# Splitting the last w2 rows of a one-token gated mix thirteen and five instead of eight and ten

## The chip, the cores and the metric

The kernel runs on one NeuronCore of one Trainium2 chip. The metric is device time in microseconds of one execution. Before the change the median of three runs is 131.49 us (131.48 to 131.57). Engines are named as in the profile: PE is TensorE, PEld its weight loads, DVE VectorE, ACT ScalarE, POOL GpSimd, SP SyncE, which here issues the large loads.

## The reference

One token `x` of 576 numbers goes through two branches, and a gate mixes them:

```python
g = sigmoid((x * gate_w).sum(-1, keepdims=True))
a = attention(x)                       # 32 heads over 16 kv heads, last 4096 keys of the cache
b = gelu(x @ w1 + b1) @ w2 + b2        # 576 -> 4608 -> 576
return g * a + (1 - g) * b
```

Inside `a`, the query is `x @ wq` (576 by 4096), the keys and values are the last 4096 positions of a cache, and the heads' outputs go through `wo` (4096 by 576). All inputs are bf16. With one token there is almost no reuse: each weight and each cache entry is read once, some 53.6 MB in all, and multiplied by a vector.

## The kernel before, in words

Everything is loaded through SP's queue in one fixed order: `w1`, `wq`, four K blocks and four V blocks of 4 MB, `wo`, then `w2`. The stages follow the loads: the first MLP layer, the query, scores and softmax per group of four kv heads, the value products, then the output projection.

The output projection is what the change touches. A "row" is a tile of 128 input features by 576 outputs; the vector that multiplies it is one column of 128 numbers (`ov` for `wo`, `gt` for `w2`, where the gate `1 - g` is already multiplied in). `wo` has 31 rows plus a four-row remainder. `w2` has `NF = 36` rows: the first half, 18 rows, comes in one load (L776), the second half in four loads (L778): rows 0 to 9, rows 10 to 14, rows 15 and 16, and row 17, counted within the second half. Row numbers below are these, 0 to 17.

A row can be added in two ways:

- `y_add` (the matmul is L389) multiplies a one-column weight by 288 outputs, twice, once per half of the 576 outputs. The two halves stand in partition 0 and partition 32 of one PSUM tile, `y_ps`. That is two weight loads and two matmuls a row.
- `y_end` (L852) writes into two other banks, `end_a` (152 columns, partitions 0 and 1) and `end_b` (136 columns, partitions 32 and 33). There the two output halves stand in two neighbouring partitions. Its weights are two columns of `g_late`, in which the column of `gt` alternates with a zero column, so that each matmul fills one partition and adds zeros to the other. A row takes four weight loads and four matmuls.

The last `LATE` rows of `w2` go through `y_end`, the others through `y_add`. When the last `y_add` is done, DVE copies `y_ps` to SBUF (`y_kept`, L845), and `y_carry` (L864) adds that copy to `end_a` and `end_b` with one f32 matmul each, which the program executes as two passes of a weight load and a matmul. At the end ACT casts `end_a` (L880), DVE casts `end_b` (L881) into `out_rows`, and SP stores the 576 numbers (L882).

The order on PE is written out by hand: `queue("pe", ...)` puts every step behind the one before. Three dummy f32 products into a spare bank (L832) stand between the stages of the projection; the last, with 256 columns, stands ahead of the second half of `w2`. SP's loads have no order against PE but through semaphores: the first matmul of each load's rows waits for that load.

The lines that set the order of the last rows:

```python
late += [(gt, f, w2_t[:, f, :]) for f in range(NJ, NF - LATE)]    # y_add
...
for j in range(LATE):
    if j == 5:
        queue("pe", y_carry)
    queue("pe", lambda: y_end(j))                                 # row NF - LATE + j
```

`g_late` has `2 * LATE + 2` columns; POOL clears it and copies the last `LATE` columns of `gt` into every second one (L480, L481).

Of the kernel before, what the change touches and what calls it, by code (L numbers as in the profile page):

```python
# [18 lines left out]
def kernel(  # L19
# [31 lines left out]
    QH = Hq * Dh // 2  # L51
    DH = D // 2
    DA = 152
    LATE = 8
    SCALE = 1.0 / (Dh**0.5)

    def first_load_ahead(nc):
# [420 lines left out]
    )  # L478
    g_late = const.tile([P, 2 * LATE + 2], BF16, name="g_late")
    nc.gpsimd.memset(g_late[:].bitcast(FP32), 0.0)  # L480
    nc.gpsimd.tensor_copy(out=g_late[:, 1 : 2 * LATE : 2], in_=gt[:, NF - LATE : NF])  # L481
    pick = const.tile([33, 2], FP32, name="pick")
# [343 lines left out]
    late += [256]  # L826
    late += [(gt, f, w2_t[:, f, :]) for f in range(NJ, NF - LATE)]
    for n, item in enumerate(late):
# [20 lines left out]
    def y_end(j):  # L849
        for s in range(2):  # L850
            for c0, c1, to in ends:
                last = nc.tensor.matmul(  # L852
                    to,
                    lhsT=g_late[:, 2 * j + 1 - s : 2 * j + 3 - s],
                    rhs=w2_t[:, NF - LATE + j, DH * s + c0 : DH * s + c1],
                    start=(j == 0 and s == 0),
                    stop=(j == LATE - 1 and s == 1),
                    skip_group_check=True,
# [14 lines left out]

    for j in range(LATE):
        if j == 5:
# [37 lines left out]
```

## Time and profile before

| | |
|---|---|
| median of 3 runs | 131.49 us |
| the profiled execution | 131.65 us |
| its span, first to last instruction | 130.4 us |
| DMA packets, bytes, mean rate | 2506, 53.69 MB, 412 GB/s |
| PE busy | 82.2 us (63%) |
| PEld busy | 26.1 us (20%) |
| DVE busy | 61.3 us (47%) |
| ACT busy, POOL busy | 11.4 us (9%), 10.5 us (8%) |
| mean granted TensorE clock | 0.869 |
| granted clock from 120 us to the end | 1.00 |

Times in the profile are counted from the span's start. Busy shares are means over stages with different limits. For the last five microseconds the table says nothing; there the timeline and the chain of waits must be read. "Landing" of a load is the moment when its semaphore has its full value, that is when the last of the 16 DMA engines has reported.

### The profile page before, as it was taken

How to read it: one execution, taken by the hardware profiler on the slowest of the kernel's cores; microseconds unless marked ns; L12 is line 12 of the kernel's file. 1: busy time of each engine (PE TensorE's matmuls, PEld its weight loads, DVE VectorE, ACT ScalarE, POOL GpSimd, SP SyncE). 2: the span in 40 equal slices, each digit the busy share in tenths (PEclk: the TensorE clock that was granted, in tenths of full speed). 3: DMA queues.
4: the chain of work that ended last, by engine and by line, in shares of the span. 5: the costliest groups of instructions: out<-in, count | busy, mean ns of one | idle time of the engine just before them, and what ended most of it. 6: DMA issues, size and time to landing. Idle time of an engine off the chain costs nothing.

```text
span 130.4 us, 1195 instructions
## 1 busy us (share of the span) xinstructions
PE 82.2 (63%) x562; PEld 26.1 (20%) x436; DVE 61.3 (47%) x51; ACT 11.4 (9%) x27; POOL 10.5 (8%) x36
## 2 busy tenths in 40 slices
PE   0003999497106998679739958951085074789995
PEld 0003111310100221211201202321032021325543
DVE  0030003416199689999999994559005005100001
ACT  3032100210300000030020003030000000000000
POOL 7019800020000000000000000000100000000000
PEclk9999999999755699999995999999658757756999
DMA  7999999899899989989989999999999989999970
GB/s 249 409 438 431 468 441 464 372 452 462 382 442 472 437 372 472 442 382 472 442 372 472 452 392 442 452 397 432 455 405 432 484 373 482 399 407 404 408 294 12
DMA packets 2506, 53.69 MB, mean 412 GB/s; under 512 B 287, under 2 KB 420, under 8 KB 710
## 3 DMA queue, kind: packets, MB, share of 16 engines
q1 hardware_dynamic: 2492, 53.61, 96.2%
q8 instruction: 4, 0.07, 0.2%
q10 hardware_dynamic: 10, 0.01, 0.0%
HBM read 53.62 MB, written 0.00 MB: 411 GB/s over the span
## 4 chain that ended last, share of the span: by engine, by line
DMA 78%; DVE 11%; PE 7%; SPq 2%; issue 0%
DMA w_t<-in_B_w_dram 29%; DMA k_t<-in_A_k_cache_dram 26%; DMA v_t<-in_A_v_cache_dram 22%; DVE kt L567 10%; PE s_ps L589 4%; PE s_ps L682 1%; DVE m L605 1%; PE end_a L852 1%; SPq L776 0%; SPq L772 0%; PE end_b L852 0%; SPq L239 0%; SPq L778 0%; SPq L235 0%; DVE out_rows L881 0%
## 5 line engine op out<-in xcount | busy, mean ns | idle before, releaser
L589 PE MATMUL s_ps<-kt,qz_flat 128*128 128x512 bf16 x128 | 32.6, 412 | 12.6 <-DVE kt L567 7.6
L567 DVE STREAM_TRANSPOSE kt<-k_t 128x4096 f32<-128x4096 f32 x8 | 35.3, 4427 | 4.3 <-DMA k_t<-in_A_k_cache_dram 2.8
L682 PE MATMUL s_ps<-v_t,pt 128*32 128x512 bf16 x96 | 9.1, 547 | 10.0 <-DMA v_t<-in_A_v_cache_dram 10.0
L589 PEld LDWEIGHTS <-qz_flat 128*128 128x128 bf16 x64 | 6.8, 107 | 35.7 <-issue 35.4
L696 DVE TENSOR_TENSOR own<-s_ps,is 128x512 f32<-128x512 f32 x3 | 2.1, 687 | 16.0 <-PE s_ps L682 16.0
L626 ACT ACTIVATE p_t<-s_ps,negm 128x1024 bf16<-128x1024 f32 x4 | 4.5, 1113 | 46.9 <-DVE negm L622 46.9
L410 PE MATMUL s_ps<-w_t,x 128*32 128x512 bf16 x36 | 6.5, 623 | 1.6 <-DVE x L352 1.6
L845 DVE COPY y_kept<-y_ps 33x288 f32<-33x288 f32 x1 | 0.5, 450 | 14.8 <-PE y_ps L389 14.8
L344 PE MATMUL xs_ps<-ident,rows 1*128 1x1 bf16 x9 | 0.6, 189 | 10.7 <-POOL ident masks.py:199 10.7
L682 PEld LDWEIGHTS <-pt 128*32 128x32 bf16 x128 | 3.7, 118 | 15.5 <-DMA v_t<-in_A_v_cache_dram 10.3
L435 DVE STREAM_TRANSPOSE turned<-s_ps 128x1024 f32<-128x1024 f32 x2 | 2.5, 1250 | 8.3 <-PE s_ps L410 8.3
L389 PE MATMUL y_ps<-wo_t,ov 128*1 128x288 bf16 x62 | 5.8, 366 | 0.6 <-DMA wo_t<-in_A_wo_dram 0.6
L638 DVE STREAM_TRANSPOSE pt<-p_t 128x1024 bf16<-128x1024 bf16 x4 | 4.9, 1224 | 2.7 <-ACT p_t L626 2.7
L410 PE MATMUL s_ps<-wq_t,x 128*32 128x512 bf16 x36 | 5.1, 624 | 0.9 <-DMA wq_t<-in_A_wq_dram 0.9
L605 DVE TENSOR_REDUCE m<-s_ps 128x1 f32<-128x1024 f32 x4 | 4.8, 1194 | 0.7 <-PE s_ps L589 0.7
L717 PE MATMUL mt_ps<-is,summed 128*128 128x8 f32 x8 | 1.8, 293 | 5.2 <-DVE summed L706 5.2
L733 POOL TENSOR_TENSOR ls<-is,sums 128x32 f32<-128x32 f32 x1 | 0.2, 243 | 58.0 <-ACT p_t L626 58.0
L358 DVE CUSTOM_DVE_ANT_0 rows<-rows 1x576 bf16<-1x576 bf16 x1 | 0.7, 745 | 8.2 <-DMA rows<-in_gate_w_dram 8.2
L389 PEld LDWEIGHTS <-ov 128*1 128x1 bf16 x62 | 3.4, 105 | 4.3 <-issue 2.1
L706 DVE TENSOR_REDUCE summed<-own 128x128 f32<-128x512 f32 x4 | 4.1, 1018 | 0.1
L832 PE MATMUL s_ps<-p_t,ones 128*128 128x512 f32 (+1 forms) x6 | 3.9, 738 | 0.0
L389 PE MATMUL y_ps<-w_t,gt 128*1 128x288 bf16 x56 | 3.8, 286 | 0.0
(95 smaller groups left out, 58.8 us busy)
## 6 DMA issues: line engine op xcount, KB each, us to landing
k_t<-in_A_k_cache_dram SPq DMA_DIRECT2D x4, 4096.0 KB, 33.0
v_t<-in_A_v_cache_dram SPq DMA_DIRECT2D x4, 4096.0 KB, 17.7
wq_t<-in_A_wq_dram SPq DMA_DIRECT2D x1, 4608.0 KB
wo_t<-in_A_wo_dram SPq DMA_DIRECT2D x1, 4464.0 KB, 28.5
w_t<-in_B_w_dram SPq DMA_DIRECT2D x1, 2880.0 KB, 14.3
w_t<-in_B_w_dram SPq DMA_DIRECT2D x1, 2592.0 KB
w_t<-in_B_w_dram SPq DMA_DIRECT2D x1, 2304.0 KB, 8.2
w_t<-in_B_w_dram SPq DMA_DIRECT2D x1, 1440.0 KB
```

Source lines behind the costliest of these rows:

```text
L389: last = nc.tensor.matmul(y_ps[32 * s : 32 * s + wide, :], lhsT=vec, rhs=row[:, DH * s : DH * s + DH], start=start, stop=stop, skip_group_ ...
L410: nc.tensor.matmul(last[n][32 * g : 32 * g + 32], lhsT=vec, rhs=part(n), start=start and g0 == 0, stop=g0 + 4 + g >= len(pieces), skip_gro ...
L435: nc.vector.transpose(out=turned[:, c0 : c0 + n], in_=src[:].rearrange("p (q l j) -> p q j l", q=q, l=32),)
L567: lambda: nc.vector.transpose(out=kt[g, f][:].bitcast(FP32), in_=keys.rearrange("p c d -> p (c d)").bitcast(FP32),),
L589: last = nc.tensor.matmul(s_ps[g][:, u * 512 : (u + 1) * 512].rearrange("p (c k) -> p c k", k=32), lhsT=qz(g, j, 2 * f + half), rhs=kv[:, ...
L605: queue("dve", lambda: nc.vector.reduce_max(out=m1[:], in_=s_ps[g][:], axis=AX.X))
L626: nc.scalar.activation(out=p_t[:].rearrange("p c k -> p (c k)"), in_=s_ps[g][:], func=ACT.Exp, bias=negm[:, 0:1], scale=SCALE, accum_out=s ...
L638: lambda: nc.vector.transpose(out=pt[:, g, :, :].rearrange("p c q -> p (c q)"), in_=p_t[:].rearrange("p c k -> p (c k)"),),
L682: last = nc.tensor.matmul(acc[g][32 * (c % 4) : 32 * (c % 4) + 32, :], lhsT=pt[:, g, c, :], rhs=v_t[g][:, c:NCK:32, :], start=(c < 4), sto ...
L696: lambda: nc.vector.tensor_tensor(out=own[:], in0=acc[g].rearrange("p (c d) -> p c d", c=4), in1=same_c.rearrange("p (c o) -> p c o", o=1) ...
L706: lambda: nc.vector.tensor_reduce(out=summed[g][:], in_=own[:].rearrange("p c d -> p d c"), axis=AX.X, op=ALU.add,),
L832: lambda: nc.tensor.matmul(spare[:, 0:item], lhsT=ones[:], rhs=p_t[:].rearrange("p c k -> p (c k)").bitcast(FP32)[:, 0:item], start=True, ...
```

## The change

Thirteen instead of eight of the last `w2` rows go to `end_a` and `end_b`.

```diff
-    LATE = 8
+    LATE = 13
```

With that, rows 0 to 4 go through `y_add` and rows 5 to 17 through `y_end`. The copy of `y_ps` stands behind row 4 and not row 9. The carry stays behind the first five `y_end` rows, which are now rows 5 to 9 and were rows 10 to 14; so it stands ahead of row 10 and not ahead of row 15. `g_late` has 28 columns and not 18, and POOL copies 13 columns into it and not 8. The loads, their sizes and their order stay as they are.

## The prediction

> **What bounds the kernel now.** I read the page's table of engines and slices first, then the chain of waits to its end, then the timeline of the last five microseconds, then stretches of it. The page:
>
> ```profile
> span 130.4 us, 1195 instructions
> PE 82.2 (63%) x562; PEld 26.1 (20%) x436; DVE 61.3 (47%) x51; ACT 11.4 (9%) x27; POOL 10.5 (8%) x36
> DMA  7999999899899989989989999999999989999970
> DMA 78%; DVE 11%; PE 7%; SPq 2%; issue 0%
> ```
>
> The loads run nearly without a pause until the last slice but one, and the chain that ended last is 78% loads. The change touches no load, so all that it can move is what stands behind the last loads. The chain's end, in order of time (start, length, what):
>
> ```profile
> 88.97 38.14 DMA w_t<-in_B_w_dram
> 127.10 0.04 issue
> 127.15 0.22 PE end_a L852
> ...
> 127.97 0.21 PE end_a L864
> 128.18 0.12 PE end_b L864
> 128.29 0.02 PE end_a L864
> 128.31 0.15 PE end_a L852
> ...
> 128.87 0.29 DVE out_rows L881
> ```
>
> The load of rows 10 to 14 lands at 127.10, PE starts on it at 127.15, and from there to the end nothing but PE, the cast and the store is on the chain: no load is waited for again. The carry (L864) is on it. The timeline of these instructions (start, length, engine, line, what, count, idle before it):
>
> ```profile
> 125.46 1.39 PE L389 MATMUL y_ps<-w_t,gt 128*1 128x288 bf16 x20
> 126.89 0.45 DVE L845 COPY y_kept<-y_ps 33x288 f32<-33x288 f32 x1 [14.78 <-PE y_ps L389]
> 127.14 0.61 PEld L852 LDWEIGHTS <-g_late 128*2 128x2 bf16 x20 [0.62 <-DMA w_t<-in_B_w_dram]
> 127.74 0.23 PE L852 MATMUL end_a<-w_t,g_late 128*2 128x152 bf16 x1
> 127.89 0.08 PEld L864 LDWEIGHTS end_a<-y_kept,pick 33*2 33x2 f32 x2
> 128.24 0.35 PEld L852 LDWEIGHTS <-g_late 128*2 128x2 bf16 x12 [0.26 <-issue]
> 128.50 0.23 PE L852 MATMUL end_a<-w_t,g_late 128*2 128x152 bf16 x1
> ```
>
> PE is out of work before 127.15, waiting for rows 10 to 14. The last of their matmuls starts at 127.74; without the carry the next row would start at about 127.80, but row 15 starts at 128.24 and row 17 at 128.50. The copy had ended at 127.34, so the carry at 127.89 waited for nothing but its turn. Were the later rows there already? The load of rows 15 and 16 is issued at 94.98 and the list of loads gives 32.8 us to landing, 127.79. For row 17 no view prints a landing, since nobody waited for it; the trace's record of that load's semaphore has its sixteenth rise at 128.13. The stretches agree (length, busy times, granted clock, DMA share, GB/s):
>
> ```profile
> 127.40:127.60 0.20, 0.20 (x13) 0.20 (x9) 0.00 (x0) 0.00 (x0) 0.00 (x0) 1.00 0.06 23
> 127.60:127.70 0.10, 0.10 (x11) 0.10 (x5) 0.00 (x0) 0.00 (x0) 0.00 (x0) 1.00 0.04 12
> 127.70:128.20 0.50, 0.50 (x13) 0.15 (x6) 0.00 (x0) 0.00 (x0) 0.00 (x0) 1.00 0.00 0
> 128.20:129.10 0.90, 0.60 (x14) 0.35 (x12) 0.23 (x1) 0.27 (x1) 0.00 (x0) 1.00 0.06 18
> ```
>
> The last weight bytes move before 127.70, at a share of 0.04 to 0.06, which is one engine of sixteen (1/16 is 0.0625). So from 127.79 the bound is PE, 0.3 to 0.4 us behind the loads, with the carry in its way.
>
> **The change part by part.** All times are those of the profiled execution (131.65 us; span 130.4). The median shown is 0.16 below it; I take the difference in time over to the median.
>
> *Steps on PE.* A `y_add` row steps on by 0.122 (ten rows: the first pair starts at 125.46, the last at 126.56, nine steps). A `y_end` row steps on by 0.13 (rows 10 to 14 start from 127.15 to 127.67, four steps; 128.24 to 128.50 for two rows). From a first `y_end` to the carry behind five rows it is 0.75 (127.15 to 127.90), 0.65 of it rows and 0.10 the change over to f32 weights. The carry holds PE for 0.34 (127.90 to 128.24).
>
> *Removed:* five `y_add` rows, 10 weight loads and 10 matmuls, 5 x 0.122 = 0.61. *Added:* five `y_end` rows, 20 and 20, 5 x 0.13 = 0.65. Net 0.04 of PE, all ahead of row 10.
>
> *The copy* moves behind row 4. Row 4's matmuls start at 125.46 + 4 x 0.122 = 125.95 and end 0.29 later, at 126.24; the copy starts 0.04 behind that (as 126.85 to 126.89 now) and ends at 126.28 + 0.45 = 126.73. DVE has nothing else there (idle 14.78 before this copy).
>
> *The carry* moves ahead of row 10. PE: rows 0 to 4 from 125.46 to 126.07, rows 5 to 9 and the change-over 0.75 to 126.82; the copy is visible at 126.73 + 0.04 = 126.77, so the carry is not held. It ends its turn at 126.82 + 0.34 = 127.16. Rows 10 to 14 are there at 127.15. The carry, its change-over and the net 0.04 (0.48 in all) thus fit into the time that PE now waits, from 126.68 (125.46 + 10 x 0.122) to 127.15, which is 0.47. If that cover were gone, they would cost 0.48, as much as the carry costs now.
>
> *Behind it:* row 10 at 127.16, five rows, 127.81. Row 15 at the later of 127.81 and its landing plus start, 127.79 + 0.045 (as 127.10 to 127.15 for row 10): 127.84. Two rows: 128.10. Row 17 at the later of 128.10 and 128.13 + 0.045 = 128.18. Now it is 128.50. From row 17 on nothing differs: four matmuls, the two casts, the store. Gain **0.32**, and what is late next is the landing of row 17. PE alone, without that wait, would reach row 17 at 127.16 + 7 x 0.13 = 128.07, so a delay of up to 0.10 ahead of row 10 costs nothing, beyond that it costs itself. The gain is at most 0.43 (128.50 to 128.07) if the loads land sooner relative to each other.
>
> *Costed at nothing:* `g_late`'s wider clearing and copy (98 ns at 15.5, 193 ns at 28.1; POOL's ten more bytes are used 98 us later). The first `y_end` now starts at 126.07 into banks whose last reader (L794, 111.27 with 0.28) has long ended. SP and POOL are passed by nothing: no DMA is issued at another place. In the store nothing changes. The granted clock is 1.00 in every stretch from 120 us on, and PE gets busier, not idler.
>
> *Added instructions:* 20 more on PE (998 weight loads and matmuls now). The page shows four instruction loads on a queue of their own, 0.07 MB, and one lies alone in the last stretch above: 0.06 of 0.90 us x 16 engines = 0.86 us of one DMA engine, starting at 128.21. The price to the kernel lies between 0 (an engine that has no weights left) and 0.86 (the engine that brings row 17 last). I take 0, and the reason: the instruction load before, at 119.05, threw one engine from the early to the late reporters (ten early and six late in `wo`'s landing, nine and seven in the next three), and that engine reports 0.5 to 0.8 before the last one each time. [...]
>
> Sum: -0.32 us, 131.65 - 0.32 = 131.33 for such a profiled execution, 131.49 - 0.32 = **131.17** for the median.
>
> **The rivals.**
>
> *A. Larger gain.* The profiled execution is 0.16 longer than the median; if the loads land closer together without the profiler, PE alone sets the pace and the gain goes to 0.43, 131.06. Against it: the landings of rows 10 to 14 and of row 17 stand 1.03 apart on the last engine, and 432 KB at the mean of 412 GB/s take 1.05.
>
> *B. The carry holds the queue.* It now stands in front of rows 10 to 17 and behind a copy with 0.05 to spare, where it had 0.55 (127.34 to 127.89). A copy that waits, or runs slower beside PE's writes, by 0.1 costs nothing, by 0.25 costs 0.15 (131.32), by 0.42 all of the gain (131.49), by more it makes the kernel slower. For it: the margin. Against it: copy and PE already ran side by side from 127.15 to 127.34, with no step of PE out of line, and 0.45 is measured there.
>
> *C. It does nothing.* If without the profiler row 17 lands 0.3 later relative to row 10, the end is already set by the load, and the carry sits in a wait: 131.49. Against it: the 0.37 between landing and start of row 17.
>
> [...]
>
> **How the numbers follow.** Forecast (131.07 to 131.25) 0.55; A 0.12; B 0.20 (a fifth of it still faster by 0.2%, a fifth slower than before); C 0.07; D 0.06. What this kernel's measurement can tell from no change is about 0.2%, 0.26 us: faster means below 131.23, slower above 131.75. Faster: 0.50 of the forecast's 0.55 + 0.12 + 0.04 = 0.66. Slower: D and the late part of B, 0.10. Same: the rest, 0.24. The range goes from 131.03 (A's 131.06 with the spread of the runs) to 131.50 (C's time, and B until the gain is gone); D and B's late part stay out, 0.10, and some hundredths of C and A on either side.
>
> **What would show it.** In the changed profile the carry should lie at 126.8, directly behind twenty `y_end` matmuls that start at 126.07, with the copy from 126.28 to 126.73; row 10 at 127.15 to 127.2; PE should show a short wait for a `w2` load ahead of row 17; from its start to the span's end, 1.9 us as now. Wrong: row 10 later than 127.26 with the carry's weight load released by DVE (B); a last landing later than 128.3 with an instruction load beside it (D); row 17 starting as late as 128.5 with the load's landing right before it (C).

## The result, and the profile after

The changed kernel takes 131.12 us (median of 9 runs, 130.95 to 131.26) beside 131.48 (131.32 to 131.57) for the kernel before, run beside it. The ratio is 0.9975, with a 95% interval from 0.9965 to 0.9985: 0.33 us by the ratio, 0.36 by the medians. The prediction was 131.17, a gain of 0.32. Measured once more, the ratio was 0.9972 (0.9961 to 0.9983).

The profiled execution after took 131.26 us, with a span of 129.9. The page, with lines as shown of before:

```profile
span 129.9 us, 1215 instructions
PE 81.3 (63%) x572; PEld 27.1 (21%) x446; DVE 61.3 (47%) x51; ACT 11.4 (9%) x27; POOL 10.5 (8%) x36
DMA  7999989899899899899899999999999998999980
```

The loads keep the engines as busy as before (413 GB/s on average, 412 before), and the counts show the ten weight loads and ten matmuls more. The timeline of the end (start, length, engine, line, what, count, idle before it; other rows between these are left out):

```profile
125.22 0.78 PE L389 MATMUL y_ps<-w_t,gt 128*1 128x288 bf16 x10 [0.46 <-DMA w_t<-in_B_w_dram]
126.04 0.45 DVE L845 COPY y_kept<-y_ps 33x288 f32<-33x288 f32 x1 [13.85 <-PE y_ps L389]
126.58 0.08 PEld L864 LDWEIGHTS end_a<-y_kept,pick 33*2 33x2 f32 x2
126.93 1.19 PEld L852 LDWEIGHTS <-g_late 128*2 128x2 bf16 x32 [0.26 <-issue]
126.98 0.23 PE L852 MATMUL end_a<-w_t,g_late 128*2 128x152 bf16 x1
127.69 0.23 PE L852 MATMUL end_a<-w_t,g_late 128*2 128x152 bf16 x1
127.88 0.37 PE L852 MATMUL end_a<-w_t,g_late 128*2 128x152 bf16 x2
128.03 0.28 PE L852 MATMUL end_b<-w_t,g_late 128*2 128x136 bf16 x2
128.36 0.27 ACT L880 CAST out_rows<-end_a 2x152 bf16<-2x152 f32 x1 [15.97 <-PE end_a L852]
128.75 0.29 SPq L882 DMA_DIRECT2D out_dram<-out_rows  x1
```

The copy runs beside rows 5 to 9, which are now end rows (rows that go through `y_end`). The carry starts at 126.58 with nothing to wait for, and PE begins to load the weights of row 10 at 126.93. That is 0.01 ahead of the landing of rows 10 to 14, which the trace's record of that load's semaphore has at 126.94; the first matmul of row 10 is at 126.98. By the same records, row 15's load lands at 127.64 and row 15 starts at 127.69. Row 17's load lands at 127.99 and row 17 starts at 128.03, as the second of the two matmuls that the line at 127.88 puts together. All three starts are 0.04 to 0.05 behind a landing, where before only row 10's was. The two profiled spans differ by 0.47: row 17 starts 0.33 nearer its landing (0.37 behind it before), and it lands 0.14 earlier in this execution.

The views do not print these waits. In the chain of waits the changed kernel's end is one run of PE from 125.22 on:

```profile
125.22 0.78 PE y_ps L389 x10
...
126.65 0.21 PE end_a L864
126.86 0.12 PE end_b L864
...
128.09 0.17 PE end_a L852 x2
...
128.37 0.02 issue
128.39 0.29 DVE out_rows L881
```

Matmuls overlap here (each lasts 0.22 to 0.23 us and they start 0.03 apart on average), so a start that is held for less than a matmul's length leaves no idle time on PE, and the chain calls it PE's. What gives it away is the gap in the starts: two matmuls into `end_a` start 0.065 apart within a load's rows, but at 127.57 and 127.69 on the step to row 15, and at 127.88 and 128.03 on the step to row 17. The experiments have to say whether the loads or PE bind there.

### The profile page after: what moved, and what is told of

It reads as the page before. It is cut to its first block, busy times and chain, and to the rows that moved or that the text cites. A ratio compares the mean times of both kernels' runs of the same rounds, so it can differ in the third digit from the quotient of the medians.

```text
span 129.9 us, 1215 instructions
## 1 busy us (share of the span) xinstructions
PE 81.3 (63%) x572; PEld 27.1 (21%) x446; DVE 61.3 (47%) x51; ACT 11.4 (9%) x27; POOL 10.5 (8%) x36
## 4 chain that ended last, share of the span: by engine, by line
DMA 63%; DVE 21%; PE 9%; issue 5%; SPq 1%; DVEq 0%
DMA k_t<-in_A_k_cache_dram 31%; DMA w_t<-in_B_w_dram 28%; DVE kt L567 16%; DMA rows<-in_A_x_dram 4%; PE s_ps L589 3%; DVE m L605 3%; DVE pt L638 2%; PE s_ps L682 1%; PE acc L682 1%; PE end_a L852 1%; PE y_ps L389 1%; PE end_b L852 1%; PE mt_ps L614 1%; DVE mr L608 1%; SPq L776 0%
## 5 line engine op out<-in xcount | busy, mean ns | idle before, releaser
L589 PE MATMUL s_ps<-kt,qz_flat 128*128 128x512 bf16 x128 | 33.1, 417 | 13.0 <-DVE kt L567 8.0
L410 PE MATMUL s_ps<-w_t,x 128*32 128x512 bf16 x36 | 5.6, 575 | 1.6 <-DVE x L352 1.6
L717 PE MATMUL mt_ps<-is,summed 128*128 128x8 f32 x8 | 2.4, 371 | 5.8 <-DVE summed L706 5.8
L389 PE MATMUL y_ps<-wo_t,ov 128*1 128x288 bf16 x62 | 4.6, 315 | 0.0
L504 DVE STREAM_TRANSPOSE q_turned<-s_ps 128x1024 f32<-128x1024 f32 x2 | 2.4, 1229 | 4.2 <-PE s_ps L410 4.2
L410 PEld LDWEIGHTS <-x 128*32 128x32 bf16 x26 | 1.4, 117 | 11.3 <-issue 6.9
```

The source lines that it names most:

```text
L389: last = nc.tensor.matmul(y_ps[32 * s : 32 * s + wide, :], lhsT=vec, rhs=row[:, DH * s : DH * s + DH], start=start, stop=stop, skip_group_ ...
L410: nc.tensor.matmul(last[n][32 * g : 32 * g + 32], lhsT=vec, rhs=part(n), start=start and g0 == 0, stop=g0 + 4 + g >= len(pieces), skip_gro ...
L589: last = nc.tensor.matmul(s_ps[g][:, u * 512 : (u + 1) * 512].rearrange("p (c k) -> p c k", k=32), lhsT=qz(g, j, 2 * f + half), rhs=kv[:, ...
```

## The experiments

The theory under test: the carry takes 0.44 us of PE with its change of weights, and the change moves it into time in which PE waits for rows 10 to 14; there it is free because the copy it needs is covered by five end rows; and then the landing of row 17 sets the end. Ratios are to the kernel before, run on the same chip. Edits are shown against the changed kernel, those with eight end rows against the kernel before. The products that the expectations call two-bank products are those of `y_add`.

**The carry back in its old place, with thirteen end rows.**

```diff
-        if j == 5:
+        if j == 10:
```

> Thirteen end rows, but the carry stands behind ten of them, ahead of row 15, where it stood before the change. Theory (the gain is the carry's place alone: ahead of row 10 it lies in PE's wait for that load, ahead of row 15 it lies on the path): the gain is gone, 131.5 us, ratio to before 0.999 to 1.001, and row 17 starts about 0.45 behind the start of row 15. Rival 1 (the gain comes from ten fewer two-bank products ahead of the copy, that is from the rows that changed sides): 131.1 us, as with the change. Rival 2 (the 20 more instructions, by shifting the last instruction load): 131.1 us too.

Measured: 131.54 us, ratio 1.0001 (0.9991 to 1.0012). The gain is gone, though five rows have changed sides and the 20 instructions are there. Its timeline:

```profile
126.88 0.61 PEld L852 LDWEIGHTS <-g_late 128*2 128x2 bf16 x19 [0.44 <-issue]
127.62 0.09 PEld L864 LDWEIGHTS end_a<-y_kept,pick 33*2 33x2 f32 x2
127.97 0.35 PEld L852 LDWEIGHTS <-g_late 128*2 128x2 bf16 x12 [0.26 <-issue]
```

Row 10 starts at 126.88, 0.04 behind its landing, the carry follows at 127.62, and row 15 starts at 127.97 although its load landed at 127.62. Row 17 starts at 128.23, 0.28 behind its landing (127.95); before the change it was 0.37. Its start is 0.26 behind row 15's and not the 0.45 that I wrote: the last matmul ahead of the carry starts at 127.47, the next would follow 0.065 later, and the carry sets it back by 0.44, ahead of row 15. So neither the rows that changed sides nor the instruction count shows a gain by itself; the place does.

**The carry a little earlier, with eight end rows.** It stands behind row 10, still ahead of row 15.

```diff
     LATE = 8
 ...
-        if j == 5:
+        if j == 1:
```

> Eight end rows as before, but the carry moved ahead, to behind the first of them (row 10), so that it stands ahead of row 15 and behind row 10's load. Theory (the carry is free only in the wait ahead of row 10, where it needs five more end rows to cover the copy): no gain, 131.5 us within 0.1, since the carry still takes its 0.44 us of PE after 127.15. Rival (it is enough that the carry does not stand directly ahead of rows 15 to 17): 131.1 to 131.2 us.

Measured: 131.45 us, ratio 0.9997 (0.9986 to 1.0008). In the timeline row 10 starts at 127.09, the carry at 127.32, and the rest:

```profile
127.09 0.09 PEld L852 LDWEIGHTS <-g_late 128*2 128x2 bf16 x4 [0.67 <-DMA w_t<-in_B_w_dram]
127.32 0.08 PEld L864 LDWEIGHTS end_a<-y_kept,pick 33*2 33x2 f32 x2
127.66 0.87 PEld L852 LDWEIGHTS <-g_late 128*2 128x2 bf16 x28 [0.26 <-issue]
```

Row 17 comes at 128.45, 0.32 behind its landing (128.13). Behind row 10 the carry costs as much as ahead of row 15, as far as the measurement can tell: in neither place does PE have free time for it.

**The carry left out, with eight and with thirteen end rows.**

```diff
-        if j == 5:
-            queue("pe", y_carry)
```

> Eight end rows as before, the carry left out, so the sum over wo and all earlier w2 rows is missing from the output. Theory: without its 0.44 us PE goes from row 14 to row 15 directly and is then held only by the landing of row 17, so this is as fast as the changed kernel: 131.05 to 131.15 us. Rival (the change also gains by something else, or the carry costs less than its place on the chain shows): 131.3 us or more.

> Thirteen end rows, the carry left out, so the sum over wo and all earlier w2 rows is missing from the output. Theory: behind the change the carry is hidden and the landing of row 17 sets the end, so leaving it out gains nothing: 131.05 to 131.15 us, within 0.05 of the changed kernel. Rival (the carry still costs part of its 0.44 us): 130.8 to 130.95 us.

Measured: 131.29 us with eight, ratio 0.9978 (0.9967 to 0.9989), and 131.25 with thirteen, ratio 0.9978 (0.9968 to 0.9989). Both medians lie 0.1 to 0.2 above what I wrote, beside 131.53 for the kernel before on the same chip, and the first is nearly at its rival's 131.3; by the ratios both are where the changed kernel is. Leaving the carry out gains 0.22% with eight end rows and nothing beyond the change with thirteen: the carry costs no time now that shows beside intervals of 0.1% either way. In the two profiles row 17 starts at 127.97 and 127.94, behind landings at 127.92 and 127.90.

**All 18 rows of the second half as end rows.**

```diff
-    LATE = 13
+    LATE = 18
```

> All 18 rows of the second half are end rows, the carry behind the first five of them (rows 0 to 4), ahead of row 5. Another 20 PE instructions, and PE's chain longer by 5 x 0.008 = 0.04 us. Theory (the end is set by row 17's landing, the carry hidden ahead of row 10): as with the change, ratio to before 0.997 to 0.998. Rival (an instruction load that comes sooner with 20 more instructions delays the last weights on its DMA engine): up to 0.86 us longer, ratio 1.000 to 1.004.

Measured: 131.04 us, ratio 0.9968 (0.9956 to 0.9980). Once more, on one chip with the changed kernel:

> The changed kernel once more, beside the next run on the same chip: ratio to before 0.997 to 0.998, 131.1 us.

> All 18 rows as end rows once more, beside the changed kernel on the same chip. Theory (row 17's landing sets the end in both): within 0.1 us of the changed kernel. Rival (18 is faster, since the copy and the carry lie a load earlier and leave PE more slack ahead of row 17): 0.1 us or more faster, ratio to before under 0.9965.

Measured: 131.10 us, ratio 0.9972 (0.9961 to 0.9983) for thirteen, and 131.24, ratio 0.9985 (0.9976 to 0.9993) for eighteen. Beside the 0.9975 of thirteen the first run puts eighteen 0.07% ahead; the second, with both on one chip, puts it 0.13% behind, 0.14 us by the medians and so more than the 0.1 that I wrote. The intervals overlap each time, so no difference is shown. The rival of the first run, a delay by the instruction load (1.000 to 1.004), is out. In its two profiles row 17 lands at 127.79 and 128.21, 0.42 apart, which is more than the change is worth: a single profile can't rank such kernels.

**The last three rows in one load.**

```diff
-    for j0, j1 in ((0, 10), (10, 15), (15, 17), (17, 18)):
+    for j0, j1 in ((0, 10), (10, 15), (15, 18)):
```

> As the change, but rows 15, 16 and 17 come in one load instead of two and one. Theory (the landing of the last load sets when PE can go on): the last landing stays, and three rows instead of one stand behind it, 2 x 0.13 = 0.26 us longer than the changed kernel, ratio to before 0.999 to 1.000. Rival (PE's chain still sets the end, the landing doesn't): no longer than the changed kernel, ratio 0.9975.

Measured: 131.43 us, ratio 0.9994 (0.9985 to 1.0002). The last landing stays (127.91), now with rows 15 and 16 in it, and PE waits visibly for it:

```profile
127.50 0.23 PE L852 MATMUL end_a<-w_t,g_late 128*2 128x152 bf16 x1
127.95 0.23 PE L852 MATMUL end_a<-w_t,g_late 128*2 128x152 bf16 x1 [0.22 <-DMA w_t<-in_B_w_dram]
```

Two more rows behind the last landing cost 0.19% beside the changed kernel's 0.9975, 0.25 us beside the 0.26 expected; the two intervals only touch. So behind the change the last landing binds: what stands behind it is paid in full.

**The carry twice**, one directly behind the other.

```diff
         if j == 5:
             queue("pe", y_carry)
+            queue("pe", y_carry)
```

> As the change, but the carry is done twice in a row, so the sum so far counts double in the output: 0.35 us more PE work ahead of row 10. In the changed kernel's profile PE would be at row 17 at 126.93 + 7 x 0.13 = 127.84 without its waits and starts it at 128.02, so 0.18 to 0.19 us of that are free. Theory: 0.16 us longer than the changed kernel, ratio to before 0.998 to 0.9995. Rival (no slack behind the carry, PE bound): 0.35 us longer, the gain all gone, ratio 1.000. Rival (much slack): ratio 0.9975.

Measured: 131.21 us, ratio 0.9982 (0.9973 to 0.9991), 0.07% or 0.09 us longer than with one, by the ratios. The second carry adds 0.26 us of PE (row 10's weights at 127.23, 0.61 behind the first carry at 126.62; with one it is 0.35), not the 0.35 that I took. Row 10 comes 0.26 behind its landing (126.97), row 17 0.13 behind its own (128.02). The difference of 0.13 to the usual 0.04, 0.09, is the loss: most of the delay is eaten by the waits ahead of rows 10, 15 and 17. The ratios rule out the rival without slack (1.000). They do not tell 0.09 from nothing, since the interval has 0.9975 in it; that there is a loss, and its size, rest on the starts of one profile.

**Less cover for the copy.** Ten end rows, the carry behind two, still ahead of row 10.

```diff
-    LATE = 13
+    LATE = 10
 ...
-        if j == 5:
+        if j == 2:
```

> Ten end rows, the carry behind the first two of them, so ahead of row 10 as with the change, but with two rows and not five between the end of the two-bank products and the carry. The copy then starts behind row 7, about 126.40 by the changed kernel's start of row 0 (125.22), and is visible at 126.89, which is 0.25 us behind PE. Theory (the place and the cover of the copy are both needed): the carry ends at 127.24, row 17 starts 0.16 us later than in the changed kernel, ratio to before 0.998 to 0.9995. Rival (the place ahead of row 10 is all): ratio 0.9975, as the changed kernel.

Measured: 131.33 us, ratio 0.9992 (0.9983 to 1.0001); its interval touches the changed kernel's only at the edge. The wait is in the timeline:

```profile
126.26 0.45 DVE L845 COPY y_kept<-y_ps 33x288 f32<-33x288 f32 x1 [14.76 <-PE y_ps L389]
126.76 0.08 PEld L864 LDWEIGHTS end_a<-y_kept,pick 33*2 33x2 f32 x2 [0.49 <-DVE y_kept L845]
126.76 0.29 PE L864 MATMUL end_a<-y_kept,pick 33*2 33x152 f32 x1 [0.29 <-DVE y_kept L845]
127.11 1.01 PEld L852 LDWEIGHTS <-g_late 128*2 128x2 bf16 x32 [0.26 <-issue]
```

PE stands idle for 0.29 until the copy is there, row 10 starts 0.35 behind its landing (126.76) and row 17 0.16 behind (127.87). By these starts row 17 is 0.12 later than in the changed kernel; the ratios say 0.22, which the intervals do not tell from it. This is the rival of the prediction in which the carry holds PE's queue. It is real, and in the changed kernel the three more rows keep it away.

**The loads of the wo remainder over 16 engines.** In the changed kernel's record nine of the sixteen DMA engines report row 17 at 126.06 to 126.64, seven at 127.58 to 127.99. I took the two small loads over 4 engines for the cause.

```diff
-    for h0, h1, at, k in ((0, 16, 0, 4), (16, Hq, 32, 4)):
+    for h0, h1, at, k in ((0, 16, 0, 16), (16, Hq, 32, 16)):
```

> As the change, but the two loads of the wo remainder, 72 KB each, go over 16 DMA engines instead of 4. In the changed kernel nine engines report row 17 at 126.06 to 126.64 and seven at 127.58 to 127.99, and two loads of 72 KB over 4 engines are 36 KB more on some. Theory (the landing of row 17 on the late engines sets the end): landings even out, the last one sooner by up to 1.07 us (the mean of all sixteen is 126.92), and with it the kernel: 0.3 to 1.0 us faster than the changed one, ratio to before 0.990 to 0.995. Rival (the end is set by PE or by all bytes together, or the late engines are late for another cause): ratio 0.997 to 0.998.

Measured: 132.97 us, ratio 1.0117 (1.0102 to 1.0131), slower than the kernel before by 1.5 us where I expected up to 1.0 us of gain; it is outside the rival's range too. Thirteen engines now report row 17 at 127.74 to 128.41, one at 129.19, two at 129.69 and 129.97. More of them are together, but later, and the last is 2.0 later. In the changed kernel the two loads land at 94.1 to 95.3. The stretch ahead of that, of this kernel (length, busy times by engine, granted clock, DMA share, GB/s):

```profile
90.00:95.00 5.00, 0.73 (x8) 0.52 (x4) 4.52 (x6) 0.00 (x0) 0.42 (x2) 1.00 1.05 337
```

and of the changed one:

```profile
90.00:95.00 5.00, 1.02 (x4) 0.89 (x4) 1.79 (x3) 0.00 (x0) 0.47 (x1) 0.50 0.99 423
```

The DMA engines are as busy (a share of 1.05 beside 0.99) and move a fifth less (337 beside 423 GB/s), where these loads pass. The two microseconds arise there: the 32 packets of 4608 bytes of these loads take 178 to 186 ns each in the changed kernel and up to 621 with 16 engines, and the last two reports of each load come at 96.8 to 97.4, where the changed kernel has its last at 95.3. A load before them has its last report at 85.3 in both kernels. Why the packets take longer, and why the seven are late in the changed kernel, stays open; the run agrees with the theory only in that a later landing of row 17 comes with a longer time.

## Why the prediction was right, point by point

*The bound.* "From 127.79 the bound is PE, 0.3 to 0.4 us behind the loads, with the carry in its way": confirmed by the two runs without the carry and by the one with the carry back in its place.

*The steps on PE.* From the start of row 0 the prediction had the carry 1.36 later and the copy's start 0.82 later; the profile after has 1.36 (125.22 to 126.58) and 0.82 (126.04). The copy took 0.45 as before, with PE writing the two other banks all the while (the `y_end` matmuls of rows 5 to 9 start from 125.83 to 126.42). From its end to the carry it is 0.09, as forecast (126.49 to 126.58; 126.73 to 126.82 in the prediction, which took 0.04 of it for the signal), so the rival B stayed away by its margin of 0.05. The start of row 0 itself was mistaken: it was taken over as 125.46, PE's turn, and came at 125.22, 0.04 behind its landing at 125.18. In the profile of before PE was 0.08 late there (125.46, 0.12 behind its landing at 125.34). Row 0 thus came 0.24 earlier and the landings 0.14 to 0.16. Had PE been as late at row 0 as before, the weights of row 10 would have been loaded from 0.07 behind its landing and row 10 would have started some 0.03 later. That lies within the slack below, so the sum did not feel it.

*The sum.* The wait ahead of row 10 just covers the carry: its weights are loaded from 126.93, and the landing is at 126.94. What is late next is the landing of row 17, as forecast: start 0.04 behind it. From row 17's start to the end of the span it is 1.9 in both. The forecast of 0.32 stands beside 0.33 by the ratio. The interval of that runs from 0.20 to 0.46, so an agreement within 0.01 is luck. The mechanism is not: row 17's start moved by 0.33 against its landing.

*The slack of 0.10 ahead of row 10.* With the doubled carry row 10 starts 0.26 behind its landing and not 0.05, so 0.21 or 0.22 later. By the starts this cost 0.09, so some 0.12 or 0.13 were free. The term was a little too small, on the safe side.

*The rivals.* A (more than 0.32, by landings closer together) is not needed: the medians give 0.36, within the interval. The argument against it had a unit wrong: 432 KB in the profile's KB of 1024 bytes take 1.07 at 412 GB/s and not 1.05, which changes nothing. C (no effect) is out. D is a last landing made later by an instruction load beside it. No run shows such a delay; the 0.06 was the author's estimate. What the profiles show is another start: the last instruction load came at 126.59 and ran until 127.59, in the midst of the last weights, where it had come at 128.21, behind them. It did no harm that can be seen:

```profile
q1 hardware_dynamic: 92, 0.12, 29.1%
q8 instruction: 1, 0.02, 5.7%
```

This is the list of DMA queues of the changed kernel from 126.55 to 127.65 (packets, MB, share). Row 17 landed at 127.99, with 128.13 before, and over all runs with the early instruction load and the data loads as in the change it landed at 127.79 to 128.21. In those where it came at the end it was 127.87 to 128.13. The semaphores say more. The sixteen reports of row 17, in their order, stand 1.05 to 1.17 behind those of rows 10 to 14, and 1.03 to 1.16 before the change, where no instruction load lies between them: none is later by anything near the 1.0 us that the instruction load takes. The conclusion "0" was right. The reason given, that its engine is done by then, is not shown, as no record names the engine.

## What to carry to other kernels

A step that only needs something early and delivers something late belongs in front of the wait that is there anyway, but it brings its own producer with it: here the carry was free only with enough rows between the end of the product and the carry to cover the copy, two rows were not enough (PE stood idle for 0.29) and five were (the copy ended 0.09 ahead of the carry). Before moving such a step, write down when every later load lands, also those that nobody waits for today, since the gain ends at the first of them: here 0.32 of a step that costs 0.44. On an engine whose instructions overlap, as the matmuls here (0.22 to 0.23 long, 0.03 apart), look at the steps between starts, not at idle time, to see which of them is held.

## What the runs showed of the hardware that was not expected

The last of the four instruction loads starts at two different places in the program. In all nine profiles of kernels with 1010 or more weight loads and matmuls on PE (thirteen and eighteen end rows, with no, one or two carries) it starts when 934 to 953 of them have started: at 126.3 to 126.6 in eight, at 128.64 in the one with later loads. With 1006 or fewer (before, its two variants and ten end rows) it comes only when 974 to 994 have started, at 127.8 to 128.4, so at the program's end. Between the kernels before and after, which differ by 20 instructions (998 and 1018 weight loads and matmuls on PE), the start moved by 1.62 us, from 128.21 with 974 of them started to 126.59 with 951. The third load, ahead of which PE's program is the same in all thirteen profiles, starts when 740 to 800 have started. No record says for which engine these loads are, and no run changed the place by itself, so the cause is not shown.
